# Weights decoded two tiles to an operation, pooled scores over 64-row blocks, another order list

## The chip, the cores and the metric

One core of a Trainium2 chip runs the whole program. The metric is the device time of one execution in microseconds, as a median of several runs.

## What is computed

A mixing layer in three parts, on a batch of 4, a length of 576 and 8 heads of width 64. Part one is an attention of two kinds whose outputs are added: a local one, in which each row sees only the rows less than 4 away, and a pooled one, in which q, k and v are averaged over 4 rows and the result is repeated 4 times. Part two is a gated convolution, part three a mixing along the sequence and a two-layer product with a ReLU. The cut reference:

```python
q_d = q.reshape(B, H, Sd, 4, D).mean(axis=3)      # k_d, v_d alike, Sd = 144
x = repeat(softmax(scale * q_d @ k_d.T) @ v_d, 4) + softmax(where(mask, scale * q @ k.T, -1e9)) @ v
h = maximum(x @ w_in, 0)                           # (B, 576, 1024)
x = h * sigmoid(conv3(h, conv_w)) @ w_out          # (B, 576, 512)
u = x + (x.T @ U @ V).T
out = u + maximum(u @ w_ch1, 0) @ w_ch2            # hidden width 2048
```

The inputs q, k and v are 32-bit. The weights are 64-bit floating point and are turned into 32-bit floats on the chip.

## The kernel before

The kernel has no loops that set the order of the work. A list of 2929 words, SEQ, is walked once (the last lines of `mixer_kernel`), and each word issues a handful of instructions: `S.3.1` issues the local scores of head pair 3 into buffer 1. Each engine runs its own instructions in the order of the list and waits only for data and for buffers that are still in use; the transfers stand in one queue, that of SyncE, in list order too. A transfer that has to wait holds up the later ones.

**Attention** goes by 16 head pairs p (two heads of 64 channels fill the 128 partitions). The words of a pair: `lq`, `lw`, `lr` load q and k, windows of v, and v by rows of four; `qs` (line 355, VectorE) sums q and k over 4 rows; `qd` (line 374, ScalarE, two operations) writes a scaled copy of the summed q into a block with zeros beside it; `S` and `Sd` (lines 390, 456) are the local and the pooled scores on TensorE; `M`, `Md` are their negated maxima (lines 405, 461). The local maxima are subtracted either by VectorE (`D`, line 412) or by TensorE (`dp`, line 419). `E`, `Ed` are the exponentials on ScalarE, `R` the row sums, `re` adds the epsilon on ScalarE, `r` is the reciprocal (line 444). `n`, `nd` normalise on GpSimd, `nv`, `ndv` on VectorE. `T`, `Td` transpose on TensorE (lines 490, 497); `c`, `cd` copy the result on ScalarE, `cv`, `cdv` on VectorE (lines 508, 514). `vs`, `vsv` sum v over four rows, on GpSimd or VectorE (lines 480, 483). `V`, `Vd` are the products with v (lines 524, 532), `xd`/`xdv` and `x` put the sum into X (line 551).

**Weights** come as tiles of 128x512 values of 8 bytes: `wl` loads one, `wd` decodes it in four steps (line 579 on ScalarE, lines 581, 583 and 586 on VectorE), `wh` and `wo`/`wO` split it into a high and a low part (line 599 on ScalarE, line 602 on GpSimd or VectorE). The raw tile and the split tile share a place, one per tile in flight. All matrix products go in three terms of high and low parts.

**Products.** `1.n.c` (line 715) is a quarter of the first product of block n (3 matmuls), `2.n.c` (line 769) a third of the second (3 matmuls). Between them stand `r1`, `c0` on ScalarE, `c1` twice on VectorE (line 742), `th`, `gt` or `gm` (line 753), `gh`, `gl` or `gL`. `%Z` hands the attention's second half of PSUM over to the products, so the first product `1.0.0` stands behind the last reader of head pair 3's result in it, `x.3`. Part three (`p`, `4`, `sr`, lines 921, 953, 866) runs from about 340 us to the end.

**Fillers.** `f.n` issues n matmuls on constants into an unused part of a PSUM buffer (line 330), and `sp` six wider ones at the start (line 312). They compute nothing that is used.

## Time and profile before

| | |
|---|---|
| time, 3 runs | median 736.92 us (736.54 to 737.19) |
| profiled execution | 738.02 us, span 736.2 us |
| granted TensorE clock, mean | 0.975 |
| TensorE (PE) | busy 714.6 us, 97% of the span |
| VectorE (DVE) | busy 464.2 us, 63% |
| ScalarE (ACT) | busy 355.3 us, 48% |
| GpSimd (POOL) | busy 186.5 us, 25% |
| transfers | 96.4 MB, mean 131 GB/s |

The span is the time from the first to the last instruction; 1.8 us of the execution lie around it. TensorE is busy nearly all of the time, so the table says what the kernel is made of, and the stretches in which TensorE is idle or runs at a lower granted clock say what could be otherwise. A busy time at a granted clock of 0.5 counts double the work's own time.

### The profile page before, as it was taken

To read this page: it belongs to the slowest core of one execution; us is meant where nothing else is said; L and a number is where in the kernel's file an instruction comes from. 1 tells how busy PE (TensorE), PEld (TensorE's weight loads), DVE (VectorE), ACT (ScalarE), POOL (GpSimd) and SP (SyncE) were. 2 spreads that over 40 slices of the span, in tenths; PEclk is the share of its full clock that TensorE was granted. 3 is DMA by queue.
4 is the path that set the end of the run, shared out by engine and by line. 5 is a ranking of instruction groups with operands and counts; after the bars stand their busy time and mean duration, and the time that the engine had idled before them with its cause. 6 is when DMAs were issued, how large, how long until landed. Compare 5 with 4: busy or idle time off the path is not lost.

```text
span 736.2 us, 14566 instructions
## 1 busy us (share of the span) xinstructions
PE 714.6 (97%) x5785; PEld 634.7 (86%) x5785; DVE 464.2 (63%) x807; ACT 355.3 (48%) x818; POOL 186.5 (25%) x186
## 2 busy tenths in 40 slices
PE   7699899999999999999999999999999999999997
PEld 5588789998988989898898898899999879999896
DVE  5898889786765655899989899752222263222223
ACT  4467567565654745688556564622221252222221
POOL 3445633342211322365623132300000021000000
PEclk9859799999999999999999999999999999999999
DMA  8886613131200000142846685573443336344412
GB/s 264 277 288 196 207 44 98 38 101 43 71 23 2 1 1 0 58 158 86 269 161 258 226 300 179 172 223 109 122 136 108 113 100 200 101 143 115 115 44 86
DMA packets 40580, 96.43 MB, mean 131 GB/s; under 512 B 4672, under 2 KB 5184, under 8 KB 40512
## 3 DMA queue, kind: packets, MB, share of 16 engines
q1 hardware_dynamic: 40512, 95.50, 39.6%
q8 instruction: 46, 0.75, 0.4%
q14 instruction: 22, 0.18, 0.1%
HBM read 76.08 MB, written 19.40 MB: 130 GB/s over the span
## 4 chain that ended last, share of the span: by engine, by line
PE 86%; DVE 4%; DMA 4%; issue 2%; ACT 2%; POOL 1%; SPq 0%; DVEq 0%; ACTq 0%; POOLq 0%
PE acc L953 25%; PE g L921 23%; PE g L715 13%; PE acc L769 12%; PE O L524 3%; DMA vr<-in_vr_dram 2%; PE S L390 1%; PE Sd L456 1%; PE O L532 1%; DMA raw<-in_w_dram 1%; PE Td L497 1%; PE h L793 1%; DVE vb L889 1%; PE T L490 1%; DMA vw<-in_vw_dram 1%
## 5 line engine op out<-in xcount | busy, mean ns | idle before, releaser
L953 PE MATMUL acc<-w,a 128*128 128x512 f32 x864 | 216.9, 393 | 0.0
L921 PE MATMUL g<-bt,as 128*128 128x384 f32 x1008 | 194.3, 337 | 0.4 <-PE g L874 0.4
L921 PEld LDWEIGHTS g<-bt,as 128*128 128x128 f32 x1008 | 178.9, 188 | 10.5 <-PE g L874 0.6
L953 PEld LDWEIGHTS acc<-w,a 128*128 128x128 f32 x864 | 159.9, 188 | 26.4
L715 PE MATMUL g<-xhl,w 128*128 128x386 f32 (+1 forms) x576 | 114.8, 344 | 0.0
L769 PE MATMUL acc<-w,ghl 128*128 128x512 f32 x432 | 110.4, 397 | 0.0
L715 PEld LDWEIGHTS g<-xhl,w 128*128 128x128 f32 x576 | 101.9, 190 | 4.2 <-issue 0.6
L930 DVE TENSOR_TENSOR tp<-g,tp 128x384 f32<-128x384 f32 x72 | 40.0, 556 | 93.3 <-ACT tp L926 51.0
L769 PEld LDWEIGHTS acc<-w,ghl 128*128 128x128 f32 x432 | 80.0, 189 | 14.9 <-issue 0.8
L926 ACT ACTIVATE tp<-g 128x384 f32<-128x384 f32 x72 | 35.2, 489 | 103.5 <-PE g L921 101.4
L941 DVE SCALAR_TENSOR_TENSOR a<-tp,a 128x384 fp32r<-128x384 f32 x72 | 41.6, 579 | 68.0 <-ACT a L937 67.6
L742 DVE SCALAR_TENSOR_TENSOR g<-h,cw,g 128x384 f32<-128x384 f32 x96 | 59.3, 618 | 27.0 <-ACT g L737 25.8
L937 ACT ACTIVATE a<-tp 128x384 fp32r<-128x384 f32 x72 | 37.7, 525 | 74.7 <-PE acc L953 54.0
L761 POOL TENSOR_TENSOR ghl<-ct,ghl 128x384 fp32r<-128x384 f32 x40 | 42.1, 1053 | 124.7 <-ACT ghl L758 120.8
L910 POOL TENSOR_TENSOR bt<-vb,bt 128x384 fp32r<-128x384 f32 x16 | 16.3, 1035 | 142.8 <-ACT bt L906 142.7
L602 POOL TENSOR_TENSOR w<-wval,w 128x512 fp32r<-128x512 f32 x20 | 27.1, 1356 | 59.2 <-ACT w L599 57.8
L583 DVE SCALAR_TENSOR_TENSOR wval<-raw,wval 128x512 uint32<-128x512 uint32 x48 | 39.4, 822 | 1.2
L721 ACT ACTIVATE h<-g 128x386 f32<-128x386 f32 (+1 forms) x48 | 23.6, 492 | 27.0 <-PE g L715 26.7
L586 DVE SCALAR_TENSOR_TENSOR wval<-raw,wval 128x512 uint32<-128x512 uint32 x48 | 35.7, 748 | 0.8
L524 PEld LDWEIGHTS O<-PT,vw 64*64 64x64 f32 x768 | 28.3, 156 | 5.4 <-issue 2.1
L579 ACT ACTIVATE wval<-raw 128x512 f32<-128x512 f32 x48 | 31.3, 665 | 3.2 <-POOL w L602 1.4
L524 PE MATMUL O<-PT,vw 64*64 64x48 f32 x768 | 30.4, 241 | 1.3 <-ACT PTd L514 1.2
(129 smaller groups left out, 862.1 us busy)
## 6 DMA issues: line engine op xcount, KB each, us to landing
as<-s SPq DMA_DIRECT2D x112, 256.0 KB, 2.8
raw<-in_w_dram SPq DMA_DIRECT2D x48, 512.0 KB, 4.3
s<-as SPq DMA_DIRECT2D x56, 256.0 KB, 3.5
qk<-in_qk_dram SPq DMA_DIRECT2D x16, 576.0 KB, 6.7
vw<-in_vw_dram SPq DMA_DIRECT2D x16, 384.0 KB, 3.1
vr<-in_vr_dram SPq DMA_DIRECT2D x16, 288.0 KB
out_dram<-u SPq DMA_DIRECT2D x17, 256.0 KB, 3.1
uvr<-in_v_dram SPq DMA_DIRECT2D x1, 576.0 KB
```

Of the source, the lines that this page charges most:

```text
L524: nc.tensor.matmul(o[rows, k, 2 * NQ * c:2 * NQ * c + 2 * NQ], e["vw"][rows, t, a], e["PT"][rows, 4 * t + a].rearrange("p j r -> p (j r)") ...
L583: eng.scalar_tensor_tensor(out=d, in0=lo, scalar=29, in1=d, op0=ALU.logical_shift_right, op1=ALU.bitwise_or)
L586: eng.scalar_tensor_tensor(out=d, in0=hi, scalar=0x80000000, in1=d, op0=ALU.bitwise_and, op1=ALU.bitwise_or)
L715: nc.tensor.matmul(gp[n][:, :wd], w[:, a, cc], xhl[g, cc][:, b, :wd], start=cc == 0 and i == 0, stop=cc == NCC - 1 and i == 2)
L742: nc.vector.scalar_tensor_tensor(out=o, in0=inner(g, hts[n], k), scalar=cw[:, k * NF + f:k * NF + f + 1], in1=o, op0=ALU.mult, op1=ALU.add)
L761: eng.tensor_tensor(ghl[n][:, 1], cts.pop(n), ghl[n][:, 0].bitcast(F32), op=ALU.subtract)
L769: nc.tensor.matmul(acc[g][c], t[:, a, c * P:(c + 1) * P], w[:, b], start=f == 0 and i == 0, stop=f == NF - 1 and i == 2)
L921: nc.tensor.matmul(o, w[:, a, k], Bs[r, j, k][:, b, :TB], start=j in (0, 1, 3) and n == 0, stop=n == 3 * HC - 1, skip_group_check=True)
L930: nc.vector.tensor_tensor(t, bank[q, 1][:, :TB], t, op=ALU.add)
L937: nc.scalar.activation(out=t[:, 0], in_=r_src(q, k), func=AF.Relu)
L941: nc.vector.scalar_tensor_tensor(out=t[:, 1], in0=r_src(q, k), scalar=0.0, in1=t[:, 0].bitcast(F32), op0=ALU.max, op1=ALU.subtract)
L953: nc.tensor.matmul(acc2[g][c], t[:, a, c * P:(c + 1) * P], w[:, b], start=f == 0 and n < 2 and i == 0, stop=f == NFP - 1 and n >= 2 and i ...
```

## The change

1. **Weights.** Two tiles form one tile of 1024 values a partition. They are still loaded by two transfers (`wl.k.j.h`), but each step of `wd` and `wh` is one operation on both: 192 `wd` words become 96, 32 `wh` words 16. `wo` stays one operation a half. The shared place is now one per two tiles, the number of decoded tiles in flight goes from 3 of 512 to 2 of 1024.
2. **Pooled scores.** `qd` is gone, with its zeroed blocks. `Sd` multiplies 64 rows of the summed q of one head with that head's summed k: 6 matmuls of 64 channels by 64 rows in place of 3 of 128 channels by 96 rows (the instructions double from 6 to 12). Of the 64 rows 48 are wanted, the rest are the next block's. The scale goes into the exponential (`Ed`) and onto the maxima, by `ns` on ScalarE (11 pairs) or `nS` on VectorE (5 pairs). `Td` transposes 128 rows in place of 96.
3. **Fillers.** The `f` words ask for 13 filler matmuls in place of 48. Seven of the 13 (`f.2`, `f.5`) stand behind a `Td`, whose wider result leaves less room: there each becomes two of a little over half the width (128 columns in place of 224).
4. **Choice of engine.** `dp` on 6 pairs in place of 3, `D` on 10 in place of 13, the epsilon on VectorE (`rE`) for 6 pairs, `cv` on 2 in place of 6, `gm` always in place of `gt` (which frees the PSUM bank earlier), and some of the low parts on other engines.
5. **The list** is a new one of 2812 words. It scores head pairs 0 and 1 together before anything else, loads the weights later, and starts the products of a block earlier against the attention. It was searched for the shortest time by the planner's nominal durations alone.
6. NAS, the number of buffers of line 866's reads, goes from 10 to 9.

The diff, cut to its core (of the list only the words ahead of the first product, and the last ones):

```diff
-SEQ = ("sf xz lq.0 z k uz wm lr.0 sp.1 lw.0 lq.1 sp.0 qs.0 sp.1 lq.2 K qd.0 vs.0.0 S.0.2 lr.1 lw.1 vs.0.1 Sd.0.1 M.0 f.1 "
-       "dp.0 Md.0 lq.3 E.0 qs.1 f.3 S.1.1 Ed.0 R.0 qd.1 M.1 re.0 f.3 Sd.1.1 lr.2 r.0 D.1 nd.0 wl.1.0 qs.2 E.1 n.0 lq.4 "
-       "vs.1.0 R.1 qd.2 f.8 T.0.0 Md.1 Td.0.2 c.0 vsv.1.1 S.2.1 Ed.1 qs.3 lr.3 lw.2 vs.2.0 cd.0 re.1 qd.3 r.1 lc ndv.1 "
...
-       "wd.1.8.1 xd.3 wo.1.7 E.5 qs.7 Ed.5 nd.4 x.3 qd.7 f.14 T.4.0 S.6.0 wd.1.8.2 %Z px.0.3 vsv.4.1 pL.0.3 lr.6 1.0.0 "
+SEQ = ("sf z k lc xz wm uz lq.0 sp.1 lq.1 lq.2 sp.0 K cw.0 cw.1 cw.2 cw.3 sp.1 lr.0 lr.1 qs.0 S.0.2 lw.0 Sd.0.1 qs.1 "
+       "S.1.1 lw.1 M.0 Md.0 Sd.1.0 lq.3 M.1 ns.0 Ed.0 qs.2 vsv.1.0 lq.4 vsv.0.0 dp.0 Md.1 wl.1.0.0 nS.1 dp.1 E.0 vsv.0.1 "
+       "vs.1.1 Ed.1 R.0 rE.0 r.0 ndv.0 lr.2 E.1 n.0 lr.3 R.1 qs.3 re.1 f.5 T.0.1 Td.0.2 wl.1.0.1 c.0 Sd.2.0 r.1 n.1 cd.0 "
...
+       "T.4.0 xd.3 S.6.0 nd.4 c.4 wl.1.6.0 x.3 wd.1.3.3 px.0.3 %Z 1.0.0 1.0.1 lr.6 pl.0.3 1.0.2 M.6 wh.1.3 lr.7 D.6 "
...
-    KPB, NAS = 3, 10
+    KPB, NAS = 3, 9
...
-    pv = ctx.enter_context(tc.tile_pool(name="pv", bufs=3, side="right", reuse_waits="tile"))
+    pv = ctx.enter_context(tc.tile_pool(name="pv", bufs=2, side="right", reuse_waits="tile"))
...
-    def q_blocks(p):
-        e = st[p]
-        e["qd"] = qds[p % 2]
-        for h in range(2):
-            rows = slice(D * h, D * h + D)
-            nc.scalar.activation(out=e["qd"][rows, :, 48 * h:48 * h + 48],
-                                 in_=e.get("sq", e["ss"])[rows, 0].rearrange("p (j r) -> p j r", j=3), func=AF.Copy, scale=SCALE / 16)
...
+        s = e["Sd"] = slot_b(n, "Sd")[:, :3 * SD].rearrange("p (j x) -> p j x", j=3)
+        ss = e["ss"].rearrange("p z x -> p (z x)")
         for j in range(3):
-            nc.tensor.matmul(s[:, j], e["qd"][:, j], e["ss"][:, 1], start=True, stop=True)
+            for h in range(2):
+                rows = slice(D * h, D * h + D)
+                nc.tensor.matmul(s[rows, j], ss[rows, 48 * j:48 * j + D], ss[rows, SD:], start=True, stop=True)
...
+    def scale_d(p, eng):
+        t = st[p]["nm"][:, 12:]
+        if eng == "ACT":
+            nc.scalar.activation(out=t, in_=t, func=AF.Copy, scale=SCALE / 16)
+        else:
+            nc.vector.tensor_scalar(out=t, in0=t, scalar1=SCALE / 16, scalar2=None, op0=ALU.mult)
...
+            nc.scalar.activation(out=t[:, j], in_=s[:, j], func=AF.Exp, scale=SCALE / 16,
+                                 bias=e["nm"][:, 12 + j:13 + j], accum_out=e["sm"][:, 12 + j:13 + j])
...
-                nc.tensor.transpose(s[:72, c, 96 * j:96 * j + 96], e["Pd"][:, j, 72 * c:72 * c + 72], ident[:96, :96])
+                nc.tensor.transpose(s[:72, c, P * j:P * j + P], e["Pd"][:, j, 72 * c:72 * c + 72], ident)
...
+    def w_load(k, j, h):
+        if h == 0:
+            t = wp.tile([P, 2, 512 * Z], U32 if Z == 2 else F32, name="raw", tag=f"w{j if k == 1 else j // 2}")
+            raws[k, j] = t.rearrange("p i (n z) -> p (i n) z", z=Z)
+        t = raws[k, j].rearrange("p n z -> p (n z)")[:, 512 * Z * h:512 * Z * h + 512 * Z]
+        src = w1[2 * j + h] if k == 1 else w2[4 * (j // 2) + j % 2 + 2 * h]
         load(t, src.bitcast(U32) if Z == 2 else src, 512)
...
+    def w_dec(k, j, step):
         if step == 0:
-            vals[k] = pv.tile([P, 512], F32, name="wval", tag="wval")
-        dec(raws[k], vals[k], step, eng)
+            vals[k, j] = pv.tile([P, 1024], F32, name="wval", tag="wval")
+        dec(raws[k, j], vals[k, j], step)
+
+    def w_hi(k, j):
+        W[k, j] = wp.tile([P, 2, 2, 512], F32R, name="w", tag=f"w{j if k == 1 else j // 2}")
+        nc.scalar.activation(out=W[k, j][:, :, 0], in_=vals[k, j].rearrange("p (i n) -> p i n", i=2), func=AF.Copy)
+
+    def w_lo(eng, k, j, h):
+        eng.tensor_tensor(W[k, j][:, h, 1], vals[k, j][:, 512 * h:512 * h + 512], W[k, j][:, h, 0].bitcast(F32), op=ALU.subtract)
```

## Rows read from the trace of the kernel before

**Rows 1.** Busy time by stretch: stretch, length, PE, PEld, DVE, ACT, POOL, PEclk, DMA, GB/s.

```profile
0.00:24.00 24.00, 18.53 (x411) 13.84 (x411) 14.53 (x22) 10.53 (x32) 9.86 (x20) 1.00 0.86 269
24.00:34.00 10.00, 7.08 (x158) 6.00 (x158) 9.15 (x18) 5.56 (x16) 1.47 (x2) 0.66 0.81 264
34.00:58.00 24.00, 20.84 (x358) 18.22 (x358) 21.53 (x36) 15.27 (x41) 13.42 (x12) 0.57 0.87 291
58.00:83.00 25.00, 21.46 (x358) 18.71 (x355) 23.17 (x39) 16.68 (x45) 15.60 (x14) 0.96 0.72 224
83.00:93.00 10.00, 10.00 (x83) 8.87 (x83) 8.06 (x14) 6.53 (x19) 6.45 (x6) 0.58 0.30 99
93.00:736.20 643.20, 636.70 (x4424) 569.08 (x4422) 387.80 (x682) 300.69 (x667) 139.70 (x135) 1.00 0.35 115
```

**Rows 2.** TensorE's waits, whole span: us in total, times, longest.

```profile
PE Td L497 <- DVE X L551: 3.7, 1, 3.7
```

**Rows 3.** Busy time by stretch, ahead of the clock's first fall; columns as Rows 1.

```profile
23.87:27.28 3.41, 0.97 (x7) 0.70 (x8) 2.57 (x7) 1.42 (x5) 0.00 (x0) 0.90 0.48 175
```

**Rows 4.** Busy time by stretch, line 330 (filler) alone: PE, PEld, PEclk, DMA, GB/s.

```profile
58.00:83.00 25.00, 3.66 (x22) 2.86 (x22) 0.96 0.72 224
```

**Rows 5.** Chain that ended last, whole span: start, us, what.

```profile
18.35 6.34 DMA vr<-in_vr_dram
...
45.33 1.68 PE Sd L456 x6
...
61.83 3.91 PE g L715 x21
...
82.98 2.80 PE O L524 x48
...
141.40 1.53 PE O L524 x48
...
146.44 2.09 PE acc L769 x9
...
246.20 2.11 PE g L715 x12
```

**Rows 6.** Chain that ended last, stretch 93 to 116.

```profile
98.07 0.50 PE Td L497 x6
...
105.75 0.65 PE O L532 x8
...
114.05 0.74 PE Sd L456 x6
```

**Rows 7.** Groups by line and shape: count, busy us, mean ns, idle before.

```profile
L742 DVE SCALAR_TENSOR_TENSOR g<-h,cw,g 128x384 f32<-128x384 f32 x96 | 59.3, 618 | 27.0 <-ACT g L737 25.8
...
L355 DVE TENSOR_REDUCE ss<-qk 128x288 f32<-128x1152 f32 x16 | 21.5, 1341 | 6.0 <-DMA qk<-in_qk_dram 3.3 <-PE Sd L456 2.5
...
L374 ACT ACTIVATE qd<-ss 64x144 f32<-64x144 f32 x32 | 10.2, 320 | 12.1 <-DVE ss L355 11.9
...
L412 DVE TENSOR_TENSOR P<-S,nm 128x384 f32<-128x384 f32 x13 | 7.2, 553 | 0.8 <-PE S L330 0.5
...
L508 DVE TENSOR_TENSOR PT<-T,front 128x576 f32<-128x576 f32 x6 | 4.5, 754 | 3.0 <-PE T L490 3.0
...
L444 DVE RECIPROCAL sm<-sm 128x15 f32<-128x15 f32 x16 | 3.9, 244 | 3.1 <-ACT sm L440 3.1
...
L480 DVE TENSOR_TENSOR vr<-vr 72x512 f32<-72x512 f32 x4 | 2.7, 681 | 1.7 <-DMA vr<-in_vr_dram 1.7
```

**Rows 8.** Tile wval, 0 to 110 us: duration ns min/median/max, first and last start.

```profile
L581 DVE TENSOR_SCALAR wval<-wval x16: 409/420/1414, 20.6 to 106.0; 128x512 uint32<-128x512 uint32 x16
L583 DVE SCALAR_TENSOR_TENSOR wval<-raw,wval x16: 674/692/2080, 21.2 to 106.5; 128x512 uint32<-128x512 uint32 x16
L586 DVE SCALAR_TENSOR_TENSOR wval<-raw,wval x15: 674/691/1736, 22.3 to 105.4; 128x512 uint32<-128x512 uint32 x15
```

**Rows 9.** Groups by line and shape, the decode of a narrower tile.

```profile
L583 DVE SCALAR_TENSOR_TENSOR uvr<-uvr 128x320 uint32<-128x320 uint32 x1 | 0.5, 481 | 0.0
```

More of the change, by code (lines that the diff above doesn't have):

```diff
@@ L277, in mixer_kernel @@
     eps = const.tile([P, 2], F32, name="eps")
-    qds = [pa.tile([P, 3, 96], F32, name=f"qd{i}") for i in range(2)]
     sms = [pa.tile([P, 15], F32, name=f"sm{i}") for i in range(3)]
@@ L299, in clear @@
             nc.gpsimd.memset(t, 1.0)
-        for t in qds:
-            nc.gpsimd.memset(t, 0.0)
     def warm():
@@ L483, in vsum, with vsum_pe, vsum_copy, eps_dve @@
             eng.tensor_tensor(d.rearrange("p h c d -> p (h c d)"), t[:, 0], t[:, 1], op=ALU.add)
+    def vsum_pe(p, n):
+        e = st[p]
+        t = e["vq"] = slot_b(n, "vq")[:72, :4 * D]
+        r = e["vr"].rearrange("p t h c d -> p t (h c d)")
+        for i in range(4):
+            nc.tensor.matmul(t, ident[:72, :72], r[:, i], start=i == 0, stop=i == 3)
+    def vsum_copy(p):
+        e = st[p]
+        d = e["vd"] = pa.tile([72, 2, 2, D], F32, name="vd", tag="vd", bufs=2)
+        nc.scalar.activation(out=d.rearrange("p h c d -> p (h c d)"), in_=e.pop("vq"), func=AF.Copy)
+    def eps_dve(p):
+        t = st[p]["sm"]
+        nc.vector.tensor_scalar(out=t, in0=t, scalar1=1e-9, scalar2=None, op0=ALU.add)
     def trans(p, n):
```

64 lines of the change are left out of this document (24 added, 40 removed), and 371 rows, old and new, of the table SEQ.

## The prediction

> **What bounds the kernel now.** I read the busy time by stretch first. From 93 us on TensorE is busy for 636.7 of 643.2 us at full clock [rows 1]; four of the 6.5 us missing are the last flush. No edit of a decode or of a score can shorten that part except by taking work off TensorE itself. What can move is the front. Up to 93 us TensorE is busy 18.53 + 7.08 + 20.84 + 21.46 + 10.00 = 77.9 us, so it is idle 15.1 us, and at the lower granted clock it loses 10 x 0.34 + 24 x 0.43 + 25 x 0.04 + 10 x 0.42 = 18.9 us more [rows 1]. So 34 us is all that a better front could give back. The chain of waits says who is late there: transfers first (the v rows that land at 24.7 us [rows 5]), then VectorE, on which TensorE's longest wait ends [rows 2]. VectorE is busy 9.15 of 10, 21.53 of 24 and 23.17 of 25 us between 24 and 83 us [rows 1]. So between 24 and 83 us the front is a VectorE problem: how much product work TensorE has been handed by the time VectorE has done its share of the attention.
>
> **The order list, the largest term.** I count words ahead of one mark, `V.5`, the sixth pair's local product, which starts at 82.98 us [rows 5] and behind which TensorE is never idle for long. In the old list 12 words `1.n.c` and 3 words `2.n.c` stand ahead of it, in the new one 20 and 6. Four `1` words take 2.11 us, three `2` words 2.09 us [rows 5]. So the new list has 8 x 0.53 + 3 x 0.70 = 6.3 us more of unavoidable work behind it at that mark. Is there room on TensorE? From 58 to 83 us it idles 3.5 us, loses 1.0 us by the clock, and spends 3.66 us on fillers [rows 1, 4], of which the new list has none behind the first product: 8.2 us, so 6.3 us fit, with little to spare.
>
> **VectorE's work ahead of the same mark**, new less old, by the words counted in the two lists and mean durations [rows 7]: one `qs` more +1.34; three first `vsv` +2.04; three `D` fewer -1.66; two `cv` fewer -1.51; four `c1` more +2.47; four `nS`/`rE` of 15 columns or fewer, priced at the reciprocal of 15, +0.98; one `cdv` and one `wO` fewer, near the 576-wide copy, -1.5; one `nv` and one `gL` fewer against one gate more, each near 0.55, -0.55; one `xdv` fewer, between the reciprocal and `D`, -0.3. Sum +1.3.
>
> Decode: the old list has 12, 11 and 10 of the three VectorE steps ahead of the mark, 12 x 0.420 + 11 x 0.692 + 10 x 0.691 = 19.6 us [rows 8]. The double step isn't in the trace. From 320 to 512 values the second step grows from 0.481 to 0.692, so 1.1 ns a value [rows 9, 8]: 512 more make 1.25 us. The first step runs at 0.420 for 512; between half of that slope and no gain at all a double one costs 0.70 to 0.84, and I take 0.70, since 0.42 for 512 is below one value per 1.1 ns. Six pairs make 6 x (0.70 + 2 x 1.25) = 19.2 us, so -0.4; with no gain at all, 6 x 2 x 1.80 = 21.7 and +2.1. In sum VectorE has **+1.0 us** (up to +3.4) ahead of the mark, for 6.3 us of TensorE work.
>
> The decode rows also hold waits: the same 512-wide step takes 0.420 at the median and 1.414 at the longest, 0.692 and 2.080 [rows 8]. Half as many operations meet half as many of these or, being longer, as many: 0 to -2.5 us in the front, taken as 0. The Trainium skill, page "SBUF — State Buffer", section "SBUF: two separate sides", says that GpSimd and VectorE hold a shared port pair exclusively for a whole instruction, and the loser blocks fully. The spread of that row is what this rule would give; it cuts both ways, as a 1.25 us step blocks GpSimd for longer too.
>
> **The other edits.** (a) `qd` goes: 32 operations of 0.320 on ScalarE [rows 7]. A pair's pooled scores start 0.65 us sooner after `qs`; `ns`/`nS` puts about 0.25 to 0.32 back between `Md` and `Ed` (0.244 for 15 columns, 0.320 for 144). ScalarE isn't full in any stretch [rows 1], so only the latency counts, and I take 0, covered by VectorE's queue; without that cover it is -0.35 a pair. (b) `Sd` costs 0.74 a pair now [rows 6]. Twelve matmuls of 64x64 with 144 columns aren't in the trace. Nearest in columns is `Vd`, 72 rows by 64, 8 in 0.65 us [rows 6], 12 of which make 0.97: +0.23 a pair. Nearest in shape is `V`, 64x64, 48 in 1.53 us [rows 5], 32 ns each for 48 columns. If the two heads' blocks run side by side, half of 0.97 is 0.49: -0.25. I take 0, as the ends lie evenly about it and neither row has both shape and columns. Eight pairs behind the mark: -2.0 to +1.8. (c) `Td` has 128 columns for 96: 0.50 a pair [rows 6] becomes 0.50 to 0.67; 0.08 each for the ten pairs behind the mark, **+0.8** (0 to 1.7). (d) `dp` for `D` on three pairs lies ahead of the mark, inside the room counted above. (e) The fillers: 35 fewer cost nothing where TensorE waits anyway; what they covered is the clock, see the first rival. (f) One place per two tiles, two decoded tiles, nine read buffers: 320 us and later, where TensorE has no waits to speak of [rows 1]. I price these at 0; if the first tiles of part three come late, TensorE waits and the cost shows at 330 to 350 us.
>
> On (b): the Trainium skill, page "TensorEngine Tiling (Array Packing)", section "Tiling Modes", says that different tiles work on weight loads and matmuls in parallel, and that a change of mode drains the array. By the first half, the sum would take the lower end of (b); the second half speaks against the edit, since `Sd` then stands between other modes. No row here has that operation.
>
> **The sum.** 738.0 (profiled execution, 736.2 of span and 1.8 around it) - 6.3 + 1.0 + 0.8 = 733.5. The profiled execution stands 1.1 us above the median of the runs, so the median comes to **732.4 us**. It leaves the lost time at the lower clock from 83 to 93 us (4.2 us [rows 1]) as it is.
>
> **Rivals.**
>
> *The clock falls earlier and stays low* (slower). In the old list TensorE's first fall follows a stretch of 3.41 us with 0.97 us busy [rows 3]. The new list has its thinnest place earlier: after `dp.1`, at about 12 us, only `f.5` stands ahead of `T.0`, which waits for `n.0` behind the sums, `R.0`, `r.0` of VectorE, about 17 us by the same durations. At half clock `V` costs 2.80 for 1.53, `Sd` 1.68 for 0.74 [rows 5, 6]; with `Td` at twice 0.50 that is 2.7 us a pair, 8.1 for the first three pairs, which the old list runs mostly at full clock. It decides from the point at which TensorE, not VectorE, is last before the products start: TensorE's work there is some 26 us in a stretch of some 40 us, so half clock throughout (52 us) would make it last. Time: 732.4 + 8.1 = 740.5. Against it: a TensorE that is last is busy, and after a busy stretch the clock came back in the old run too (0.57 up to 58 us, 0.96 after [rows 1]).
>
> *The waits stay* (no change). `V.5` isn't set by VectorE's sum but by its order and by transfers, which take 0.86 and 0.87 of the DMA engines up to 58 us [rows 1]; both lists load nearly as much ahead of the first product, 16.2 and 16.4 MiB. Then the 3.5 us of idle time from 58 to 83 us stay, and only the fillers' room is filled: 732.4 + 3.5 = 735.9, with its spread up to 738.4. For it: the chain's transfers [rows 5]. Against it: those the attention's first four pairs need are earlier than that in both lists.
>
> *Better than the sum.* With more products at hand TensorE doesn't run dry ahead of 83 us, the clock doesn't fall there, and 4.2 us more come back: 728.2; with the lower end of (b), 726.2.
>
> **Chances.** The forecast, 729.5 to 735.4: 0.42. Better: 0.15. The waits stay, 735.4 to 738.4: 0.20. Clock falls earlier, above 738.4: 0.23. A measurement of this kernel tells 0.2% from no change, about 1.5 us, so faster 0.57, same 0.20, slower 0.23. The range from 726 to 741 takes in the ends of (b), (c) and the decode, the better case and the clock's, and leaves out some 0.05 below and 0.13 above. Of the forecast alone the range is 729.5 to 735.4.
>
> **What would show it.** First product at 57 to 60 us (now 61.83 [rows 5]). TensorE's idle time from 58 us to 83 us under 1.5 us, and 20 and 6 product words ahead of `V.5` at 83 to 85 us. Decode steps of 0.70 and 1.25 us. `Sd` at 0.49 to 0.97 us a pair. Granted clock above 0.57 from 34 to 58 us. The prediction is wrong if the clock is at 0.5 from 17 us on, if the first product comes after 62 us, or if TensorE waits anywhere between 100 and 480 us, in part three's first tiles above all.

## The result, and the profile after

The changed kernel takes **738.14 us** (median of 20 runs, 734.56 to 745.03), the kernel before on the same chip 735.71 (20 runs, 731.26 to 738.63). The ratio of the runs is 1.0055, with a 95% interval from 1.0032 to 1.0079: slower, by 2.4 us between the medians and by about 0.5%, some 4 us, between the runs as a whole. On a second chip it is 738.30 against 735.43, ratio 1.0037 (1.0009 to 1.0066). The forecast, 732.4, had the sign wrong; its range, 726 to 741, holds the time.

A warning comes first. The profiled execution of the changed kernel took 736.25 us with a span of 734.3, which is *less* than the 738.0 and 736.2 of the one before. The two kernels spread by 7 and 10 us from run to run. Before was traced on one of its slower runs, the changed kernel on one of its faster ones. Whoever compares only these two traces explains a gain that isn't there. So the same kernels were traced again below, and only what all traces of a kernel share is read as its own.

Busy time by stretch in the changed kernel, columns as in [rows 1]:

```profile
0.00:24.00 24.00, 19.93 (x377) 14.33 (x378) 15.40 (x28) 7.90 (x25) 5.08 (x14) 0.86 0.86 258
24.00:34.00 10.00, 7.25 (x204) 5.95 (x203) 8.27 (x12) 6.72 (x22) 2.85 (x3) 1.00 0.88 297
34.00:58.00 24.00, 20.27 (x393) 16.70 (x389) 21.17 (x28) 13.16 (x28) 15.99 (x12) 0.64 0.90 286
58.00:83.00 25.00, 24.69 (x380) 21.15 (x377) 24.75 (x33) 18.09 (x44) 19.47 (x16) 1.00 0.66 201
83.00:93.00 10.00, 10.00 (x108) 8.65 (x107) 9.74 (x16) 9.14 (x22) 7.41 (x7) 1.00 0.45 146
93.00:734.30 641.30, 634.00 (x4427) 563.51 (x4425) 370.84 (x615) 288.62 (x617) 157.88 (x152) 1.00 0.35 115
```

Against [rows 1], the waits between 58 and 83 us have gone (24.69 us busy of 25, 21.46 before) and the clock stands at 1.00 from 83 to 93 us (0.58 before). ScalarE and VectorE have lost work over the whole span, as meant: 343.6 and 450.2 us busy against 355.3 and 464.2. None of this shows in the median.

TensorE's waits over the whole span, where before a wait of 3.7 us on VectorE stood [rows 2]:

```profile
PE Sd L442 <- issue: 2.9, 2, 1.5
PE O L534 <- issue: 2.4, 1, 2.4
PE S L366 <- DVE X L561: 2.0, 1, 2.0
...
PE S L320 <- DVE nm L388: 1.3, 1, 1.3
PE S L320 <- ACT P L413: 1.2, 1, 1.2
```

The longest waits end on "issue": TensorE waited for nothing that the profile shows. In the kernel before such waits make 1.7 us in this trace's counterpart and none in a second one; the last experiments turn on them.

The two marks of the prediction in the order of time (start us, us): the first product, and the sixth pair's local product `V.5`.

```profile
61.05 2.02 PE L720 MATMUL g<-xhl,w 128*128 128x386 f32 x10
...
85.26 1.60 PE L534 MATMUL O<-PT,vw 64*64 64x48 f32 x48
```

And what the pooled scores cost TensorE at full clock, in the chain of waits, where [rows 6] had 0.50 and 0.74:

```profile
108.03 0.66 PE Td L506 x6
...
110.10 0.88 PE Sd L442 x12
```

### The profile page after: what moved, and what is told of

It reads as the page before. It is cut to its first block, busy times and chain, and to the rows that moved or that the text cites. A ratio compares the mean times of both kernels' runs of the same rounds, so it can differ in the third digit from the quotient of the medians.

```text
span 734.3 us, 14586 instructions
## 1 busy us (share of the span) xinstructions
PE 716.1 (98%) x5868; PEld 630.3 (86%) x5868; DVE 450.2 (61%) x726; ACT 343.6 (47%) x753; POOL 208.7 (28%) x203
## 4 chain that ended last, share of the span: by engine, by line
PE 91%; DVE 3%; DMA 2%; ACT 1%; issue 1%; POOL 0%; SPq 0%; DVEq 0%; ACTq 0%; POOLq 0%
PE acc L960 26%; PE g L928 24%; PE g L720 14%; PE acc L774 13%; PE O L534 3%; PE Sd L442 2%; PE Td L506 2%; PE S L373 2%; PE h L798 1%; PE O L542 1%; DMA vr<-in_vr_dram 1%; PE g L881 1%; PE T L499 1%; PE mx L819 1%; DMA qk<-in_qk_dram 1%
## 5 line engine op out<-in xcount | busy, mean ns | idle before, releaser
L774 PE MATMUL acc<-w,ghl 128*128 128x512 f32 x432 | 112.3, 400 | 0.0
L766 POOL TENSOR_TENSOR ghl<-ct,ghl 128x384 fp32r<-128x384 f32 x48 | 52.1, 1085 | 107.5 <-ACT ghl L763 107.4
L917 POOL TENSOR_TENSOR bt<-vb,bt 128x384 fp32r<-128x384 f32 x20 | 21.5, 1092 | 149.1 <-ACT bt L913 147.6
L607 POOL TENSOR_TENSOR w<-wval,w 128x512 fp32r<-128x512 f32 x20 | 29.6, 1487 | 38.5 <-ACT w L604 38.4
L763 ACT ACTIVATE ghl<-ct 128x384 fp32r<-128x384 f32 x48 | 25.0, 521 | 18.7 <-DVE ct L758 10.1
L758 DVE SCALAR_TENSOR_TENSOR ct<-g,h 128x384 f32<-128x384 f32 x48 | 26.5, 552 | 11.6 <-ACT g L751 8.2
L594 DVE SCALAR_TENSOR_TENSOR wval<-raw,wval 128x1024 uint32<-128x1024 uint32 x24 | 33.4, 1397 | 0.2
L534 PEld LDWEIGHTS O<-PT,vw 64*64 64x64 f32 x768 | 26.4, 145 | 6.9 <-issue 5.5
L751 ACT ACTIVATE g<-g 128x384 f32<-128x384 f32 x48 | 22.8, 476 | 19.8 <-DVE g L747 19.6
```

Source lines behind the costliest of these rows:

```text
L534: nc.tensor.matmul(o[rows, k, 2 * NQ * c:2 * NQ * c + 2 * NQ], e["vw"][rows, t, a], e["PT"][rows, 4 * t + a].rearrange("p j r -> p (j r)") ...
L594: nc.vector.scalar_tensor_tensor(out=d, in0=hi, scalar=0x80000000, in1=d, op0=ALU.bitwise_and, op1=ALU.bitwise_or)
L766: eng.tensor_tensor(ghl[n][:, 1], cts.pop(n), ghl[n][:, 0].bitcast(F32), op=ALU.subtract)
L774: nc.tensor.matmul(acc[g][c], t[:, a, c * P:(c + 1) * P], w[:, b], start=f == 0 and i == 0, stop=f == NF - 1 and i == 2)
```

## One account for all runs

Every kernel below is read with the same division of its trace at `V.5`. **Work** is the time in which a matmul record of TensorE runs, times the granted clock; **idle** is the time in which none runs; **lost** is the rest, what the lower clock costs. Left of the bar stands what lies ahead of `V.5`, right of it what lies behind, idle and lost in one sum. **First** is the start of the first product. **Issue** is the sum of the waits of that name ahead of 110 us. The last 4.1 to 4.5 us of each span, behind TensorE's last product, stand in no column. All in us.

```
                            span  first   V.5 at | work  idle  lost | work behind  idle+lost | issue
before                     736.2  61.76    82.98 | 54.5  15.1  13.3 |   642.5         6.6    |  1.7
before, second trace       733.2  59.21    80.12 | 55.0  15.8   9.4 |   642.7         6.3    |  0.0
before, few fillers        733.4  61.56    82.18 | 50.3  14.5  17.4 |   643.6         3.5    |  0.0
changed                    734.3  61.05    85.26 | 64.3  10.9  10.1 |   640.0         4.7    |  5.3
changed, second trace      732.3  62.16    86.93 | 63.6  11.8  11.5 |   640.1         1.0    |  5.0
changed, third trace       737.7  65.33    89.19 | 63.9  16.0   9.3 |   639.5         4.7    |  7.5
changed, fourth trace      734.1  61.07    84.92 | 64.5  13.2   7.2 |   640.1         4.8    |  5.4
e1  new scores, old order  737.4  62.52    82.89 | 57.2  11.7  14.0 |   646.5         3.8    |  0.6
e2  changed, narrow decode 740.4  67.98    92.98 | 63.9  18.5  10.6 |   640.3         2.7    |  7.5
e3  changed, more fillers  740.5  67.90    91.59 | 67.5  12.9  11.2 |   639.9         4.7    |  4.6
e4  changed, D for dp      737.3  64.87    88.32 | 61.4  14.4  12.6 |   639.9         4.7    |  6.4
e5  changed, old scores    739.3  69.52    94.03 | 59.8  23.6  10.6 |   637.9         2.9    |  4.3
e7  new order alone        743.7  67.13    93.68 | 60.6  19.2  13.8 |   638.3         7.2    |  3.2
e8  both parts, old front  748.9  68.13    92.39 | 57.0  17.5  17.9 |   646.1         6.3    |  1.0
e9  wide decode, old front 745.4  69.70    93.17 | 54.5  19.3  19.4 |   643.4         4.7    |  0.9
e12 products moved behind  742.2  64.90    86.69 | 58.0  19.9   8.8 |   647.3         3.8    |  8.3
e14 sums on GpSimd         733.7  61.18    85.04 | 64.3  14.7   6.1 |   639.6         4.7    |  5.6
e15 650 KB under way       734.3  64.49    88.33 | 63.7  15.0   9.7 |   640.6         1.0    |  6.9
e16 450 KB under way       746.6  71.15    95.63 | 64.1  19.9  11.6 |   641.0         5.6    |  4.5
e17 code shifted           736.0  63.41    87.27 | 63.1  13.8  10.4 |   639.7         4.7    |  5.2
```

Three things stand out. Work behind `V.5` is a constant of each program, to within 0.6 us between traces, and it adds up to within about a microsecond: 642.6 (mean of the two traces of the kernel before) - 6.3 for the moved products + 2.7 for eight `Sd` at 0.14 and ten `Td` at 0.16 gives 639.0, and the four traces of the changed kernel have 639.5 to 640.1. What varies from run to run is how late `V.5` comes, 80.1 and 83.0 us before and 84.9 to 89.2 in the changed kernel, and what is idle and lost behind it, 1.0 to 4.8 us in the traces of the changed kernel.

The third is where `V.5` is lost, 5.0 us between the means (86.6 and 81.6). The first product starts at 61.8 and 59.2 us before and at 61.1 to 65.3 after, 1.9 us later in the mean. From there to `V.5` it is 21.2 and 20.9 us before and 23.9 to 24.8 after, 3.1 us more. That stretch by itself, in the first trace of either kernel, columns as in [rows 1]; the second line is the fillers (line 330) alone, with PE, PEld, PEclk, DMA and GB/s:

```profile
61.76:82.98 21.22, 17.86 (x246) 15.48 (x238) 19.39 (x35) 13.90 (x35) 12.24 (x11) 0.96 0.81 247
61.76:82.98 21.22, 1.48 (x7) 1.03 (x7) 0.96 0.81 247
...
61.05:85.26 24.21, 23.90 (x284) 20.34 (x277) 23.92 (x33) 17.69 (x42) 19.83 (x16) 1.00 0.58 175
```

TensorE, idle for 3.4 us of it before, is idle for 0.3 us or less in all four traces of the changed kernel. In the other runs under the new order the stretch takes 23.5 to 25.0 us, but for e7 and e12, so nearly all that they differ by ahead of `V.5` lies ahead of the first product.

## The experiments

The first theory was that TensorE pays more for the pooled scores than forecast. Its rivals: the order list, the fillers and the clock, the decode.

**e1, the new pooled scores alone, under the old code and order.**

```
-  "qd": q_blocks, ... words qd.0 to qd.15
+  ns.p right behind each Md.p
-      nc.tensor.matmul(s[:, j], e["qd"][:, j], e["ss"][:, 1], start=True, stop=True)
+      for h in range(2): nc.tensor.matmul(s[rows, j], ss[rows, 48 * j:48 * j + D], ss[rows, SD:], ...)
       and the 128-row maxima, exponentials, transposes and copies that go with it
```

> The old kernel and its order list, with the pooled scores alone changed: 64-row blocks, no scaled copy of q, the maxima scaled by ns on ScalarE behind each Md, Td over 128 rows. Theory 1 (TensorE pays): in the profile of the changed kernel Sd takes 0.88 us a pair for 0.74 and Td 0.66 for 0.50, so 0.30 us a pair, and from about the sixth pair on TensorE is never idle: 10 to 16 pairs, 3.0 to 4.8 us slower than the old kernel, 1.004 to 1.0065. Theory 2 (the clock and the fillers lose the time): within 1 us of the old kernel, since its fillers stay. Theory 3 (the new list's order loses it): the same, within 1 us.

Measured: 738.33 us (737.08 to 741.91) against 734.17, ratio 1.0064 (1.0042 to 1.0086). Its chain has the changed kernel's prices:

```profile
111.58 0.88 PE Sd L456 x12
123.37 0.66 PE Td L497 x6
```

`V.5` stands where it stood in the first trace before (82.89), work behind it is 3.9 us more, and the whole is 4.2 us longer. In this order the new pooled scores are a loss, of about the size of TensorE's added work. At 0.14 a pair in `Sd` and 0.16 in `Td`, eight and ten pairs make 2.7 of the 3.9 us; what the other 1.2 are was not found. The fillers behind a `Td` change with it here too, two of 128 columns for one of 224.

**e2, the changed kernel with the decode back to 512 values a step.**

```
-      dec(raws[k, j], vals[k, j], step)
+      for h in range(2): dec(raws[k, j][:, 512*h:512*h+512], vals[k, j][:, 512*h:512*h+512], step)
       and the step that makes the high part likewise
```

> The changed kernel with its own list, but each decode step and each high part issued as two operations of 512 values in place of one of 1024. Theory 1 (TensorE pays; the wide decode helps VectorE a little): 0 to 2.5 us slower than the changed kernel, so 1.003 to 1.009 of the old one. Rival (the wide steps are what hurts, since they hold up what stands behind them on VectorE and what shares GpSimd's port): 1 to 3 us faster than the changed kernel, 0.999 to 1.002 of the old one.

Measured: 744.43 us (740.73 to 747.27), ratio 1.0138 (1.0100 to 1.0175): 6 us slower than the changed kernel. `V.5` comes at 92.98, and the first product, at 67.98, is as late already. In this order the two-tile decode is worth more than forecast. The steps of the changed kernel themselves cost what was estimated (ns min/median/max):

```profile
L589 DVE TENSOR_SCALAR wval<-wval x8: 680/774/4230, 27.5 to 95.7; 128x1024 uint32<-128x1024 uint32 x8
L591 DVE SCALAR_TENSOR_TENSOR wval<-raw,wval x8: 1211/1226/1905, 30.0 to 104.0; 128x1024 uint32<-128x1024 uint32 x8
L594 DVE SCALAR_TENSOR_TENSOR wval<-raw,wval x8: 1206/1224/3698, 32.4 to 105.5; 128x1024 uint32<-128x1024 uint32 x8
```

0.68, 1.21 and 1.21 at the least, for 0.70 and twice 1.25.

**e3, more fillers, and e4, D for dp**, both in the changed kernel's list. A filler is a product that TensorE does while it waits; `dp` is the shift of the scores done on TensorE, `D` the same on VectorE.

```
e3   f.5 ... f.2 ... f.1 ... f.5   ->   f.18 ... f.8 ... f.6 ... f.8
e4   dp.3 ... dp.4 ... dp.7        ->   D.3 ... D.4 ... D.7
```

> The changed kernel with 40 filler words in place of 13, at the four places where its list has any (18, 8, 6, 8; those behind a Td count double at 128 columns). Theory 2 (the clock): the granted clock stays up in the front, 2 to 4 us faster than the changed kernel, 0.998 to 1.001 of the old one, and the runs lie closer together. Theory 1: the front's waits hide the fillers or not, 0 to 2 us slower than the changed kernel, 1.003 to 1.008 of the old one, and as wide a spread.

> The changed kernel with the local maxima of pairs 3, 4 and 7 subtracted by VectorE (D) as the old list does for them, in place of TensorE (dp). It takes 3 x about 0.8 us off TensorE and puts 3 x 0.55 us on VectorE. Theory 1 (TensorE pays): 1 to 2.4 us faster than the changed kernel, 1.000 to 1.003 of the old one. Rival (VectorE still sets the front): 0 to 1.7 us slower than the changed kernel, 1.003 to 1.007 of the old one.

Measured: e3 742.44 (736.28 to 745.03), ratio 1.0094 (1.0060 to 1.0128); e4 740.21 (734.39 to 742.39), ratio 1.0073 (1.0046 to 1.0099). Neither helps. e3 added 3 us of work ahead of `V.5`, which came later. e4 took 2.7 us of work off TensorE, gave VectorE three `D` for it, and gained nothing. **Few fillers under the old order** is the counterpart:

```
f.1 f.3 f.3 f.8 f.2 f.10 f.14 f.6 f.1   ->   f.1 f.1 f.1 f.2 f.1 f.2 f.3 f.1 f.1
```

> The kernel before with 13 filler words' worth of products ahead of the mark where it has more, about as few as the new list; nothing else changed. Theory 'fillers keep the clock up and are worth their time': 1 to 4 us slower than the kernel before, with a lower granted clock in 34 to 83 us. Rival (fillers only fill waits): within 1 us.

Measured: 735.27 (731.19 to 739.52) against 735.43, ratio 1.0002 (0.9979 to 1.0026). Ahead of `V.5` there is 4 us less work and 4 us more lost to the clock than in the first trace. So as far as one trace tells, the fillers pay for themselves in clock and no more, and their number doesn't explain the loss.

**e5, the changed kernel with the old pooled scores; e7, the new order with neither part.** To find room for `qd` in SBUF, both keep one `qd` and one `xd` buffer and a single copy of the identity matrix. `qd.p` stands behind `qs.p`.

```
e5   ns, nS out; qd.p in; Sd as 3 products of 128x96, Td of 96 rows; one buffer of qd and xd
e7   e5, and the decode in steps of 512 as in e2
```

> The changed kernel with the old pooled scores put back: the scaled, zero-padded copy of q on ScalarE (qd), three products of 128x96 a pair, 96-row transposes; wide decode and the new order list stay. One qd buffer instead of two, one xd buffer, and the identity matrix kept once, to make room. Theory (the 64-row pooled scores cost TensorE 0.14 us a pair in Sd and 0.16 in Td, 16 pairs): 3 to 5 us below the changed kernel, 733 to 735 where that has 738, about at the kernel before; Sd back at 0.74 us and Td at 0.50 a pair at full clock. Rival (the list is what costs; the pooled scores' extra TensorE time lies under waits on VectorE): within 1.5 us of the changed kernel, and about 0.5% above the kernel before. Second rival (the qd step of 0.6 us on ScalarE, the copy that the change removed, is worth more than the TensorE time): slower than the changed kernel.

> The new order list with neither part of the change: old pooled scores and decode in steps of 512. With the three other kernels it gives each part's worth twice. Theory (parts add): 6 us above the run with only the old pooled scores, since undoing the wide decode cost 6 us in the new list, so 739 to 741, and 3 to 5 below the run with only the decode undone. Rival (the wide decode's worth came from VectorE time that the new nS and Sd maxima took): undoing it costs under 3 us here, 735 to 737.

Measured: e5 742.32 (739.01 to 744.86), ratio 1.0108 (1.0073 to 1.0144); e7 749.53 (745.38 to 752.27), ratio 1.0195 (1.0157 to 1.0232). The theory missed badly on e5: giving back 0.30 us a pair made the kernel 4 us *slower* than the changed one (738.30 on the same chip). Work behind `V.5` did fall, to 637.9, but `V.5` came at 94.0. Undoing the decode as well cost 7 us more, as in e2; but e7 is 5 us above e2, where parts that add would put it 3 to 5 below. One buffer for two did add waits of its own. In e5, up to 75 us, ScalarE's longest wait in sum is for `Sd` to have read the one `qd`, and e7 has 9.3 us of the same; in the kernel before, with two, there is none:

```profile
ACT qd L368 <- PE Sd L451: 9.9, 5, 4.1
```

So the two-tile decode is worth 6 to 7 us under the new order, twice measured. What the new pooled scores or the order by themselves are worth, e5 and e7 don't show.

**e8 and e9, the old order up to the last decode step of part one**, with both parts and with the decode alone. A two-tile step stands where the second tile's step stood; behind that point the new order follows. e9 has e5's buffers.

```
e8   changed code; words of the old order up to wO.1.7.1, wd.1.2j.s dropped, wd.1.(2j+1).s -> wd.1.j.s
e9   the same order with e5's code
```

> Both parts of the change (two-tile decode, 64-row pooled scores, no scaled copy of q) under the order of the kernel before, up to the last decode step of part one; behind that the new order. A two-tile step stands where the second tile's step stood; ns stands right behind each Md; the fillers are those of before. Theory (the new order costs nothing by itself; the loss is TensorE's extra work in the pooled scores): as slow as the changed kernel or slower, 737 to 741. Rival (the loss comes from the new order's front): back at the kernel before or below it, 731 to 735.

> Part one of the change alone under the order of the kernel before: two-tile decode, old pooled scores with the scaled copy of q, the order of before up to the last decode step of part one, the new order behind it. Theory (parts add: the new pooled scores cost 4 us in the old order, the two-tile decode saved 6 in the new one): 728 to 732, the best of all. Rival (the two-tile steps hold VectorE for up to 1.2 us at a time and come later than the first tile's steps did, so what stands behind them starts late): no gain, 734 to 739.

Measured: e8 748.25 (744.97 to 753.86), ratio 1.0211 (1.0163 to 1.0258); e9 746.86 (745.19 to 747.63), ratio 1.0182 (1.0145 to 1.0219). Both expectations failed, and by a lot. "Parts add" is refuted: the two-tile decode is worth 6 to 7 us in the order that came with it and costs some 10 in the other, placed as it is here (e8 against e1, ratios 1.0211 and 1.0064; e9 against the kernel before 13, with the one buffer of e5 in it). Another place for the steps in the old order was not tried. TensorE's longest waits in e8, ahead of 110 us, are on VectorE:

```profile
PE Td L504 <- DVE P L393: 4.0, 1, 4.0
PE Td L504 <- DVE X L559: 2.4, 1, 2.4
PE T L497 <- DVE P L430: 1.8, 1, 1.8
```

From here the question was why, in the order that suits it, the changed kernel's `V.5` still comes late.

**The changed kernel and the kernel before, traced again.**

> The changed kernel itself once more, beside the others on the same chip, for a second trace. All theories: about 738, 0.4 to 0.7% above the kernel before. If the front (before the last weight of part one, mark V.5) is where the loss lies, this trace shows V.5 at 85 to 90 us and, past V.5, the same work within 1 us as in the first trace.

> The changed kernel, one more trace. Both earlier traces (734.3 and 732.3 us of span) are below the median span of its runs, 736.2. If waits in the front make its spread, a trace above the median has TensorE idle for more than 10.8 us ahead of 83 us of the span (the first trace's sum) and the same work behind it.

> The changed kernel, a fourth trace, for the same reading: a span above 736 us goes with more than 10.8 us of idle TensorE time ahead of 83 us; one below with less. Past 110 us of the span the idle time stays under 1.5 us in either.

> The kernel before, one more trace, since the first (736.2 us of span) is among the slower of its runs. Expected: a span of 730 to 735, V.5 at 82 to 84 as in the first, and, past it, TensorE work of 642 to 643 us at full clock with 0 to 2 us lost to half clock instead of 4.2.

Measured: the changed kernel 738.30 (733.36 to 742.00) beside 735.43; single executions of 739.71 and 736.12; the kernel before 734.95. In the third trace, the only one above the median span, TensorE is idle 16.0 us ahead of 83 us, as expected, and the second has `V.5` at 86.93, within the 85 to 90 expected. The rest misses: 11.8 us idle with a span of 732.3, 13.2 with 734.1, so idle time alone doesn't order the runs, and the fourth trace has 3.2 us idle past 110 us for the 1.5 expected. In the work behind the mark all agree. The kernel before has `V.5` at 80.12 in its second trace, not 82 to 84, and 3.2 us lost behind it, not 0 to 2.

**e12, the moved products put back behind `V.5`.** This tests the largest term of the forecast. Up to the first product the list is that of the changed kernel.

```
-  1.3.0 ... 1.3.3  2.1.0  r1.3  c0.3  2.1.1  1.4.0 ... 1.4.3  c1.3.1  c1.3.2  2.1.2   ahead of V.5.0
+  the same words right behind V.5.0
```

> The changed kernel with 8 of its words 1 (1.3, 1.4) and 3 of its words 2 (2.1), and the ScalarE and VectorE steps that hang on them, moved from ahead of the mark V.5 to right behind it, so that as many stand ahead as in the kernel before (12 and 3). Theory (the front is set by VectorE and ScalarE, so products there fill waits and are worth their 6.3 us): V.5 comes no earlier than 83, the whole 3 to 7 us slower, 741 to 745. Rival (in the front TensorE's own work sets the end as much, so they only lengthen it): V.5 comes 3 to 6 us earlier, at 80 to 84 against a mean of 86.6 in four traces of the changed kernel, and the whole is within 1.5 us, 737 to 740.

Measured: 742.43 (740.50 to 744.90), ratio 1.0107 (1.0074 to 1.0139), 4 to 5 us slower than the changed kernel. `V.5` starts at 86.69 us without the products ahead of it, at a mean of 86.6 with them:

```profile
86.69 2.17 PE L532 MATMUL O<-PT,vw 64*64 64x48 f32 x48
```

Both numbers are those of the theory, but that `V.5` stands where it stood is chance: in this trace the first product comes at 64.90, 2.5 us above the mean of 62.4, with the same words ahead of it. From there to `V.5` it is 21.79 us, 2.4 less than the 24.2 of the changed kernel, and TensorE has 2.5 us idle in it again. So the products fill waits in part, about 4 of their 6.3 us, and for the rest they push `V.5` back.

**e14, three sums of pooled values from VectorE back to GpSimd.**

```
vsv.1.0 ... vsv.2.0 ... vsv.3.0   ->   vs.1.0 ... vs.2.0 ... vs.3.0
```

> The changed kernel with three of the five sums of the pooled values that the new order gives VectorE ahead of the mark (vsv.1.0, vsv.2.0, vsv.3.0: 0.69 us each on VectorE) given to GpSimd (1.28 us each), as the kernel before has more of them there. Theory (VectorE's own work, 2.5 us more of it ahead of V.5 than in the kernel before, sets the front): V.5 1.5 to 3 us earlier and the whole 1 to 3 us faster than the changed kernel, 735 to 737. Rival (GpSimd's longer steps hold up VectorE, or the waits are on another engine or on transfers): no gain, 737.5 to 741, V.5 at 85 to 90.

Measured: 739.97 (734.87 to 744.99), ratio 1.0108 (1.0067 to 1.0148). No gain; the one trace has `V.5` at 85.04, inside the four of the changed kernel. VectorE is busy 69.1 us ahead of `V.5`, where those have 70.0 to 71.8, so the edit did what it says. Nothing here says that VectorE's amount of work sets the mark.

**e15 and e16, fewer transfers under way.** In the traces of the new order TensorE stands still at the same places of its program, behind its 223rd, 349th, 476th, 729th or 857th matmul record, about 126 apart or a multiple of it, mostly in the middle of a run of products. It goes on 1.3 to 1.5 us after a 16 KB packet of the instruction queue has landed. The page lists that queue:

```profile
q8 instruction: 46, 0.75, 0.4%
```

0.75 MB in 46 packets is 16 KB each. In the third trace (start us, us, engine, line, what, idle before) one stop is 3.57 us long:

```profile
10.20 0.70 PE L442 MATMUL Sd<-ss 64*64 64x144 f32 x7
13.44 0.98 PE L442 MATMUL Sd<-ss 64*64 64x144 f32 x5 [2.54 <-issue]
...
21.59 0.90 PE L373 MATMUL S<-qk 64*24 64x32 f32 x84
26.06 0.27 PE L373 MATMUL S<-qk 64*24 64x32 f32 x12 [3.57 <-issue]
```

There the packets run from 10.75 to 11.93 us and from 23.69 to 24.76 us. In the kernel before the first one comes at 10.20 us as well, when TensorE is at record 117, so that none of it is waited for:

```profile
12.59 0.60 PE L330 MATMUL S<-mask,identR 128*128 128x224 f32 x3 [0.67 <-DVE nm L405]
13.03 0.90 PE L456 MATMUL Sd<-ss,qd 128*96 128x144 f32 x6
13.84 1.15 PE L330 MATMUL S<-mask,identR 128*128 128x224 f32 x8
```

The theory tried was that the packets queue behind the data.

```
-    WAY, NLIM = 900, 44
+    WAY, NLIM = 650, 44      (e16: 450)
```

> The changed kernel with 650 instead of 900 KB as the limit from which SP holds the next of the first 44 loads back, nothing else changed. In its four traces TensorE stands still in the front for 5.0 to 7.5 us in waits that the page calls issue, always at the same places of its program (its 224th, 350th, 477th, 730th, 972nd matmul, about 126 apart), and goes on when a 16 KB packet of the instruction queue has come; in two traces of the kernel before these waits are 1.5 and 0 us. Theory (instruction packets queue behind the data transfers under way): with fewer under way the issue waits fall below 3.5 us, V.5 comes at 82 to 85 instead of a mean of 86.6, and the whole is 1 to 4 us faster than the changed kernel (734 to 737). Rival (the front is short of data, so that fewer transfers under way make loads land later): no faster, 738 to 742.

> The same with 450 KB, about one transfer under way at a time. Theory: the issue waits fall further, below 2 us; but loads come one after another, and waits on transfers take their place, so the whole is between the run with 650 KB and 742. Rival: issue waits as with 900 KB, 5 us or more, and the whole above 740.

Measured: e15 736.14 (731.50 to 741.22), ratio 1.0015 (0.9984 to 1.0047); e16 745.40 (743.21 to 748.94), ratio 1.0163 (1.0130 to 1.0197). e15 looks 2 us faster than the changed kernel, though the intervals overlap. But its trace has 6.9 us of issue waits and `V.5` at 88.3, so it is not faster by the mechanism that was named. e16 has fewer issue waits (4.5), but VectorE waits 6.2 us for q and k up to 72 us, where the changed kernel's first trace has 1.9. The theory is not borne out.

**e17, the same program 42 records further on in the code.** Each warming word becomes eight short products in place of one long one.

```
-        nc.tensor.matmul(slot_b(n, "spin"), t[:, :P], t, start=True, stop=True)
+        o = slot_b(n, "spin")
+        for i in range(8):
+            nc.tensor.matmul(o[:32, 64*i:64*i+64], t[:, :32], t[:, 64*i:64*i+64], start=True, stop=True)
```

> The changed kernel, where each of the three warming words sp (one product of 128x128 with 512 columns, 2 records) is made of eight products of 32 weight columns with 64 columns (16 records). The rest of the program is the same, but stands 42 TensorE records later in the code, so that the places where TensorE waits for its instructions (the 224th, 350th, 477th, 730th, 972nd record) fall on other work, 42 records earlier in it. Theory (those waits come from where such a place falls: in or right behind runs of short products after a wait): the issue waits change by more than 2 us in sum and move to other tiles, while the record numbers stay; the whole moves by 1 to 4 us, faster if the sum falls below 3.5 us, slower if it rises. Rival (the waits belong to the work, Sd and S, and not to the place in the code): the same tiles wait as long as before, at record numbers 42 higher, and the whole stays within 1 us of the changed kernel, 737 to 739.5.

Measured: 739.08 (736.74 to 740.58), ratio 1.0075 (1.0049 to 1.0102). The stops stayed at records 223 and 476 and moved to other tiles:

```profile
8.97 0.70 PE L375 MATMUL S<-qk 64*24 64x32 f32 x61
12.29 0.57 PE L375 MATMUL S<-qk 64*24 64x32 f32 x35 [2.62 <-issue]
12.80 1.70 PE L444 MATMUL Sd<-ss 64*64 64x144 f32 x12
```

`Sd` now runs through, `S` is cut. So these waits belong to a place in the code, not to the operation that is cut. Some shorter ones, all ahead of `T`, went with their work: records 545 and 971 in the third trace became 587 and 1013, so they are of another kind. The sum of all is unchanged (5.2), and the time is within a microsecond of the changed kernel. As the sum didn't move, this run can't say what it is worth.

The traces say a little more. The stop behind record 349 lasts 3.57 us in the third trace, 3.14 in e12 and 3.30 in e15, and their first products come at 65.33, 64.90 and 64.49 us. In the other three traces of the changed kernel and in e14 it lasts 0.8 us or less, and the first product comes at 61.05 to 62.16, much as before (59.2 and 61.8). So the long stop goes with a first product some 3 us later. That is seen in seven traces; no run switched the stop on or off.

No version tried beats the kernel before.

## Why the prediction was wrong, step by step

**What bounds the kernel: right in the main.** Nearly all that these kernels differ by lies ahead of `V.5` or is counted work behind it; the rest is 1 to 7 us idle and lost behind it.

**The moved products, -6.3, and the room of 8.2 us for them: the first step that failed.** The work did leave the part behind the mark, to within a microsecond of the count. But the room was counted from 58 us, and the products can't use what lies ahead of the first of them, at 61.8. From there to `V.5` the kernel before has 3.4 us idle, 0.7 lost to the clock and 1.5 of fillers, 5.6 us in place of 8.2. TensorE's work there at full clock rises from 17.2 us, fillers included, to 23.1 to 23.9, and the stretch becomes 3.1 us longer. An idle time under 1.5 us from 58 to 83 was to show that the room was there; the 0.3 us of the first trace (2.0 in the second, all of it ahead of its first product) show that it was used up. e12 agrees from the other side: without the products the stretch is 2.4 us shorter. They are worth 4 to 5 us, not 6.3.

**(b), `Sd` taken at 0: wrong in size.** It measured +0.14 a pair, inside the ends of -0.25 and +0.23. The nearer row was `Vd`, 81 ns for each product; the new ones take 73 ns (0.88 / 12), the old ones 123 (0.74 / 6). The hoped-for case that two heads' blocks run side by side would have been 0.49. The page "TensorEngine Tiling (Array Packing)", section "Tiling Modes", of the Trainium skill says that different tiles work in parallel; here 12 of them take longer than the 6 of full height that they replace; how much of the 73 ns is overlap, this row can't tell.

**(c), `Td` at 0.08 a pair: half of it.** It measured 0.16, in proportion to the columns (128/96 of 0.50 is 0.67), the upper end that was left aside. Together, for eight and ten pairs, (b) and (c) are 2.7 us behind the mark instead of 0.8, and e1 shows 4.2 for the whole.

**VectorE's +1.0 us ahead of the mark: the other step that failed.** `V.5` was put at 83 to 85 us; it comes at 85.26 in the trace beside the result, and at a mean of 86.6 in four, against 81.6 in two of the kernel before. That is 5.0 us, beyond the upper bound of 3.4 too. 3.1 of them are the room above. The other 1.9 lie ahead of the first product, which was forecast at 57 to 60 us and comes at 62.4 in the mean, in two of the four past the 62 that was to show the prediction wrong. The count of VectorE's work was not far off: VectorE is busy 70.0 to 71.8 us ahead of the mark, 68.4 and 68.1 before, so 2.5 more for 1.0 (up to 3.4). What failed is the assumption that the mark follows VectorE's sum. Behind the first product TensorE is the one that never waits. Ahead of it e4 gave VectorE three more `D` and e14 took about 2 us from it, without a clear change either way, though one trace each says little beside a spread of 4.3 us. There the engines and the transfers wait for one another in turn, and a sum of one engine's durations doesn't price that. The rows that ought to have warned are VectorE's own: it is idle for 9.5 of the first 24 us and for 5.2 of the next 59 [rows 1], so it was never the whole bound.

**In sum**: -6.3 + 2.7 + 5.0 = +1.4 where -4.5 was forecast; the medians say +2.4. Idle and lost time behind the mark is 2.7 us less in the changed kernel's traces (mean 3.8 for 6.5), and the work there 0.9 more than counted, so that the traces alone make about nothing (mean spans 734.6 and 734.7). The rest is in runs that weren't traced: the four traces lie 1.6 us below the median span of the kernel's runs, the two of the kernel before 0.8 above theirs, and 5 of the changed kernel's first 20 runs took 741 us or more. What happens in those was not seen.

**The base.** 738.0 was taken to stand 1.1 us above the median; over 20 runs it stands 2.3 above. Three runs were too few for that.

**Why the first product comes later is not settled.** The issue waits, 4.5 to 8.3 us in the new order with the new pooled scores and 0 to 1.7 in the old, are larger than the gap, and the traces with a long one at record 349 are the late ones. But no run took them away, so that they are the cause is argued and not shown. e5 and e7, with fewer of them (4.3 and 3.2), are slower still, by waits of their own.

**The rivals.** *The clock falls earlier and stays low* was right in its first half. The first fall comes at 13.5 us in the first trace (0.86 in the first 24 us), at 26.6 before (inside the stretch of [rows 3], not behind it, as the prediction read that row). But it doesn't stay: 21.9 to 27.8 us at half clock in four traces, 37.5 and 28.8 in two of before. *The waits stay* has the measured time in its range, 735.4 to 738.4, and its premise, that order and transfers and not VectorE's sum set `V.5`, fits what lies ahead of the first product. But the waits that it meant are gone, 24.69 us busy of 25, so that its number came out is luck. *Better than the sum* had the clock from 83 to 93 us right (1.00); the later mark and the wait that follows ate the gain.

**The shared port**, which the prediction cited from the page "SBUF — State Buffer", section "SBUF: two separate sides", of the Trainium skill, shows in the open, and it is a cost that the prediction took as 0. VectorE's first decode step, 0.68 us by itself, and GpSimd's steps beside it (start us, us):

```profile
95.72 4.23 DVE L589 TENSOR_SCALAR wval<-wval 128x1024 uint32<-128x1024 uint32 x1
```

```profile
95.61 1.29 POOL L473 TENSOR_TENSOR vr<-vr 72x512 f32<-72x512 f32 x1
96.85 2.54 POOL L607 TENSOR_TENSOR w<-wval,w 128x512 fp32r<-128x512 f32 x2
99.35 1.17 POOL L476 TENSOR_TENSOR vd<-vr 72x256 f32<-72x256 f32 x1
```

It starts 0.11 us after the first of four steps of GpSimd that follow one another without a gap, and ends 0.56 us after the third. `X` (L561) waits behind it on VectorE, TensorE's 2.0 us wait ends on `X`, a wait between 100 and 480 us as it was to show the prediction wrong, and 3.4 us at half clock follow it. This agrees with the page's rule that the loser blocks; that it may lose three times in a row the prediction didn't consider. In the second trace the same step starts 0.25 us ahead of the same step of GpSimd, and it is GpSimd's that gets longer:

```profile
97.02 0.84 DVE L589 TENSOR_SCALAR wval<-wval 128x1024 uint32<-128x1024 uint32 x1
97.27 1.74 POOL L473 TENSOR_TENSOR vr<-vr 72x512 f32<-72x512 f32 x1
```

There TensorE has no wait on `X`, and 1.0 us is idle and lost behind `V.5`. In the other three, with 4.20 to 4.23 us for the step, it is 4.7 or 4.8; e3, e4, e14 and e17, with 3.6 to 4.2 us, have 4.7, and e15, with 0.69, has 1.0. So which of the two starts first, by a tenth or a quarter of a microsecond, goes with 3.7 us, about what the two kernels differ by.

## What to carry to other kernels

When a kernel runs from an order list that was searched for it, an edit has no price of its own: the two-tile decode was worth 6 to 7 us under one order and cost some 10 under the other, where it was put. Count the room for moved work only from where that work can start, and with all else that the edit puts there. Divide the trace at marks, here the first product and `V.5`. Behind the second, counted work adds up to within about a microsecond; ahead of it sum no single engine, and trace each kernel several times before believing a difference of 1%.

## What the chip showed that was not expected

- TensorE stops at fixed numbers of its matmul records (223, 349, 476, 729), up to 4.1 us at a time, until a 16 KB packet of the instruction queue lands. The profile calls it "issue". The packet is waited for when TensorE gets there early: in the changed kernel it reached record 222 at 10.6 to 11.2 us, in the kernel before at 13.3.
- The time at half clock, from each run's span and mean granted clock, goes with the order too: medians of 23 to 32 us for the kernel before in its sets of runs, 24 and 25 for the changed one, 37 and 38 in e7 and e5, 46 and 51 in e8 and e9. In e8 and e9, half of what is over 30 makes 8 to 10 of the 13 to 15 us that they lose. What sets it was not tried.
- A VectorE step of 0.68 us takes 4.20 to 4.23 us in three traces where it starts just behind a step of GpSimd, and 0.84 in the one where it starts just ahead of it.
- Twelve products of 64x64 take 0.88 us where six of 128x96 with the same 144 columns take 0.74.
